# Pooled attention and a three-way maxout layer on one core: another order of all steps, and stores split by 128-token halves

## The chip, the core and the metric

The kernel runs on one core of one Trainium2 chip. The metric is the device time of one execution in microseconds (us); less is better. A core has five engines that run at once: TensorE (PE; its weight loads are shown as PEld), VectorE (DVE), ScalarE (ACT), GpSimd (POOL) and SyncE (SP). SP, POOL and ACT also issue DMAs, which share 16 DMA engines. Each engine runs its instructions in the order in which the program gives them and waits at semaphores for others.

## What is computed

```python
# B, H, S, D = 8, 8, 576, 64; pool = 8; Sp = 72
k_p = k.reshape(B, H, Sp, pool, D).mean(axis=3)
v_p = v.reshape(B, H, Sp, pool, D).mean(axis=3)
scores = scale * np.matmul(q, k_p.transpose(0, 1, 3, 2))
attn = np.exp(scores - max); attn = attn / (sum + 1e-09)
x = matmul(attn, v_p)  ->  4608 tokens x 512            # heads side by side
h = np.maximum(np.maximum(x @ w1, x @ w2), x @ w3)      # 4608 x 768
out = h @ w_out                                         # 4608 x 512
```

## The kernel before

There are two kinds of work. **Attention** goes batch by batch (8 of them, 576 tokens each), the **layer** goes by blocks of 512 tokens (9 of them, n = 0 to 8). Everything is written out by hand: the first batch and the first block stand in Python code ahead of line 869, the last output block (`out_last`) behind line 901, and all between comes from one long text, `ORDER` (L879). `run` (L829) reads it word by word and emits each step's instructions for all engines. So a word's place sets the place of its instructions on PE, DVE, ACT, POOL and SP alike.

The words, with b a batch and i a part of it:

- `<kb`, `<vb`, `<qb`: a load of 576 KB, issued by POOL (`load_k` L86, `load_v` L97, `load_q` L109). A load is made to wait for the last matmul ahead of it in the order and for the last DMA transpose ahead of it. Each of k, v and q has two buffers.
- `Kb` twice (DVE): folds eight key rows to two, a fold of 96x1536 and one of 96x768; `kb` (L207): six matmuls on PE that turn the folded keys, and four copies to `kz`.
- `Vb` seven times: four pieces `half<-vt` (L807) and two pieces `vt<-half` (L811) on POOL, then the sum `vp<-vt` on DVE. Each POOL piece waits for the last of DVE's sums that stands ahead of it (`piece`, L816).
- `qbi` (batches 1 and 2): q is transposed on PE and copied out to `qT` by ACT, or, as for every word with a star, by DVE (`move`, L77). `Tb` three times (batches 3 to 7): the same by DMA transposes, issued by SP (L305). There are two `qT` buffers.
- `sbi`, i = 0 to 8 (`scores_flat`, L237): 512 columns of scores on PE into `psf` (two buffers), exp on ACT into `et`. The first of a batch reads what the first T wrote.
- `vbi`, i = 0 to 4 (`values`, L267): eight matmuls into `pav` (one buffer), a reciprocal and a product on DVE that give `xn`, 128 tokens of x. `xbi` turns it into `xT` by PE and a copy for b up to 2; for b over 2, `v` itself issues a DMA transpose on SP (L256). `xT` is a ring of 2048 tokens.
- `p`: half a piece of block 0's output, with a copy to `osb` in every second one.
- `A` to `H` with 1 to 4 (`two_products`, L657): the hidden layer of n = 1 to 3, four matmuls of 512 or eight of 256 columns; ACT takes one product's positive part, DVE the maximum. They take and give back four PSUM banks (`take`, `give`, L524).
- Blocks 4 to 8 get the hidden layer with seven products in place of eight (`hidden_product`, L614): `1a` to `7c`, four matmuls of 256 columns each, from sums of x (`t1` to `t4`, tile `xs`, on DVE) and of the weights (`f`, `F`, on DVE, once). All output blocks go the same way (`out_product`, L712): `1d` to `7d`, ten matmuls of 256 columns, from sums of h (`u1` to `u4`, tile `hs`) and of the weights (`S`, `G`). Products 1, 2, 3, 5 and 6 are moved by ACT or, starred, by DVE; 4 and the later of 5 and 7 are added by DVE. Each block has two tiles `osb` of 2 x 128 tokens; there are three such buffers.
- `store` (L685) writes one such tile out: tokens of one position in the nine-fold interleave lie 64 to a group, so a tile holds four groups, u = 0, 1 in partition halves and m = 0, 1 in the free direction. It issues a DMA for each u, over both m where their places in the output allow it, else one for each u and m. All are on SP, in order with the transposes.

`out_last` (L745) does the last block in halves m of 128 tokens, 14 products of five matmuls, the last two being `(4, 0)` and `(4, 1)`.

Of the kernel before, what the change touches and what calls it, by code (L numbers as in the profile page):

```python
# [14 lines left out]
def kernel(  # L15
# [11 lines left out]
    nc = tc.nc  # L27
# [3 lines left out]
    B, H, S, D = q.shape  # L31
# [10 lines left out]
    NG = 9  # L42
    GS = (0, 2, 4, 6, 8, 1, 3, 5, 7)
# [18 lines left out]
    def psum(shape, dtype, name, tag, bufs):  # L62
        return pools[-1].tile(shape, dtype, name=name, tag=tag, bufs=bufs)
# [5 lines left out]
    def matmul(*args, **kw):  # L69
        latest[0] = nc.tensor.matmul(*args, **kw)  # L70
        return latest[0]
# [66 lines left out]
    for sign in (1, -1):  # L138
        nc.gpsimd.affine_select(
            out=pick, in_=pick, compare_op=ALU.is_ge, fill=0.0, base=7 * (sign < 0),  # L140
            pattern=[[sign, 6], [-8 * sign, 128]], channel_multiplier=6 * sign)
    for i in range(3):
        load_w(slice(256 * i, 256 * i + 256))
    nc.gpsimd.dma_start(
        out=wo_sb, in_=moe_w_out.rearrange("(jc p) c -> p jc c", p=128))
# [378 lines left out]
    def take(key, shape=(128, 2, 256)):  # L524
        i = free_banks.pop(0)
        taken[key] = i, psum(list(shape), F32, name="pb", tag=f"pb{i}", bufs=1)
        return taken[key][1]

    def give(key):
        free_banks.append(taken.pop(key)[0])  # L530
# [80 lines left out]
    def of(i):  # L611
        return "B" if i == 2 else "C" if i in (4, 7) else "A"
# [69 lines left out]
            nc.vector.tensor_tensor(out=hTs[n][:, j, c], in0=relus[j], in1=b, op=ALU.max)  # L682
        give("n")

    def store(e, n, j, o, c):  # L685
        for u in range(2):
            b, g = divmod(2 * (4 * n + 2 * j) + u, NG)
            pair = g + 2 < NG and GS[g + 2] == GS[g] + 4
            for m in range(0, 2, 1 + pair):
                b, g = divmod(2 * (4 * n + 2 * j + m) + u, NG)  # L690
                dst = out[S * b:S * b + S, :].rearrange("(r g) c -> r g c", g=NG)
                e.dma_start(out=dst[:, GS[g]:GS[g] + 4 * pair + 1:4, c],  # L692
                            in_=o[64 * u:64 * u + 64, m:m + 1 + pair, c])

    def out_operands(n, i, m, r):
        za, zb = PRODUCTS[i]
        c = slice(128 * m, 128 * m + 128)
        if isinstance(zb, str):
            z = int(zb[1]) - 1
            left = xs[n % 2][:, z, r, c] if r < 2 else ths[n][:, z, r - 2, c]  # L700
        else:
            at = HALF * (zb % 2) + 128 * m
            left = (tokens(NB * n + at, NB * n + at + 128)[:, 2 * (zb // 2) + r] if r < 2
                    else hTs[n][:, JH * (zb // 2) + r - 2, at:at + 128])
        h, r = (0, r) if r < 2 else (1, r - 2)
        right = so[h][:, int(za[1]) - 1, r] if isinstance(za, str) else out_w(za, h)[:, r]
        return left, right

    outs = {}
    lo, hi = slice(0, HALF), slice(HALF, C)  # L710

    def out_product(n, i):  # L712
# [27 lines left out]
        if i in (5, 7, 3) and all((n, z, "d") in done for z in (5, 7, 3)):  # L740
            store(nc.sync, n, 1, o(1), slice(0, C))
        if i in (2, 4) and all((n, z, "d") in done for z in (2, 4)):
            store(nc.sync, n, 0, o(0), slice(0, C))

    def out_last(n):  # L745

        o = sb2.tile([128, 2304], F32, name="ob", tag="et")[:, 0:2048].rearrange(
            "p (j m c) -> p j m c", j=2, m=2)
        banks, ended = {}, set()

        def product(i, m):
            f = of(i)
            if (f, m) not in banks:
                banks[f, m] = (psum([128, HALF], F32, name="oC", tag=SC[0], bufs=SC[1])
                               if f == "C" else take((f, m), (128, HALF)))
            p = banks[f, m]
            for r in range(5):
                matmul(p, *out_operands(n, i, m, r), stop=(r == 4),
                                 start=(i in FIRST and r == 0), skip_group_check=True)
            ended.add((i, m))  # L760

            def plus(j, c):
                nc.vector.tensor_tensor(out=o[:, j, m, c], in0=o[:, j, m, c],  # L763
                                        in1=banks["B" if c == lo else "C", m], op=ALU.add)

            def both_of(*parts):
                return all((z, k) in ended for z in parts for k in range(2))

            if i in (1, 5, 6, 3):
                nc.scalar.copy(out=o[:, int(i in (5, 3)), m, lo if i in (1, 3) else hi],  # L770
                               in_=p)
            elif i == 2:
                plus(0, lo)
            elif i == 4:
                plus(0, hi)
            if i in (5, 7) and (12 - i, m) in ended:
                plus(1, hi)
            if i in (2, 3):
                give((f, m))
            if i in (5, 7) and both_of(5, 7):  # L780
                store(nc.sync, n, 1, o[:, 1], hi)
            if i == 3 and both_of(3):
                store(nc.scalar, n, 1, o[:, 1], lo)
            if i in (2, 4) and both_of(i):
                store((nc.gpsimd, nc.sync)[i // 4], n, 0, o[:, 0], (lo, hi)[i // 4])

        return product

# [88 lines left out]
    for _ in range(SC[1]):  # L877
        psum([128, NB], F32, "psf", *SC)
    ORDER = """  # L879
        q12* q13 V1 p s10 s11 p* s12 V1 s13 p s14 q20* s15 V1 s16 V1 V1 p* s17 V1 s18 K2 V1  # L880
        <k3 p K2 q21 q22 <q3 V2 v10 V2 q23 V2 k2 v11 x10* <q4 p x11* v12 s20 p s21 V2 V2 V2
        s22 v13 H3 <v3 s23 s24 <k4 v14 V3 C3 s25 f x13 f B3 T3 V2 K3 x12 T3 E3 T3 G s26 K3
        s27 A4 V3 s28 t1 C4 T4 x14 v20 A3 S S T4 T4 D4 v21 x20 V3 D3 B4 x21 k3 v22 t3 u1 E4
        H4 V3 V3 <v4 v23 x22 p S G A1 H1 V3 A2 v24 s30 s31 K4 1d s32 s33 H2 s34 C1 K4 <q5
        x23* G s35 <k5 C2 t2 s36 s37 V3 t3 D1 t1 u2 s38 D2 k4 <v5 S u3 x24 G v30 E1 6d* V4
        s40 s41 t2 B1 s42 t4 v31 V4 u4 s43 V4 B2 s44 v32 s45 5d s46 F v33 s47 E2 T5 s48 V4
        V4 v34 7d u1 2d V4 V5 u3 <k6 K5 F V5 u2 3d 4d 1d K5 7d V4 t1 V5 2d <k7 6d* k5 v40 T5
        C1 V5 t4 C2 s50 s51 v41 V5 V5 T5 E1 H1 E2 v42 <q6 H2 5d u4 f B1 F D1 V5 f D2 4d B2
        K6 t2 K6 3d t3 A1 A2 F <v6 1a t1 1b <q7 s52 t2 u1 s53 v43 2a 2b K7 V6 s54 6b 6a s55
        u3 K7 s56 v44 1d s57 t4 5a s58 V6 u2 V6 2d t3 t4 3a u4 v50 k7 7b 5b* 6d T6 v51 7a 3b  # L890
        k6 4b T6 5d 4a T6 7d 1c T7 3d 2c 6c 4d t1 V6 V6 <v7 t2 5c T7 1a T7 v52 7c s60 s61 2a
        3c s62 s63 6a v53 s64 4c 1b 5a s65 s66 v54 2b 3a s70 6b 1d s67 t3 u1 u2 u3 u4 t4 s68
        5b 2d 7b V6 6d V6 V7 7a 4b 3b s71 v60 4a 1c 5d 6c* 2c s72 V7 v61 s73 7c s74 5c s75
        7d s76 V7 v62 3c s77 4c t1 4d 3d t2 u1 1d t4 u2 V7 v63 s78 t3 1a 2d u3 2a 6a 1b* 6d*
        2b v64 V7 V7 5a V7 6b 7a 3a 5d v70 5b 4a 7b v71 3b 3d u4 1c 4b 7d t1 t2 6c 7c 2c 5c
        4d 3c 1a 4c v72 1b 2a 6a 6b u1 u2 2b 5a u4 t4 v73 1d 5b u3 3a t3 6d v74 3b 2d* 7b 7a
        5d 4b 4a 7d t1 1c 3d 6c* 2c t3 4d t2 1a t4 5c 7c 2a 3c 6a 4c 1b 5a 7a 6b 2b 4a 5b 1c
        u1 3a 3b 2c u2 6c u4 u3 1d 7b 5c 6d* 4b 3c 2d 5d 7c 7d 4c 3d 4d
    """

    run(ORDER)
# [36 lines left out]
```

## Time and profile before

| | us |
|---|---|
| runs | 230.5, 229.07, 233.97; median 230.5 |
| the profiled execution | 227.75 |
| its span | 225.9, granted clock 0.997 |
| PE busy from 38.20 to 216.95 us | 174.01 of 178.75 |
| DVE busy there | 153.45 |
| ACT busy there | 113.12 |
| POOL busy there | 62.32 |

The steps of `ORDER` run from about 38 us to about 213.7. Matmuls are pipelined and the ends that the profile gives them are modelled, so PE's busy time counts some of its waiting as work; the starts of its matmuls are what tells. The page's costliest groups, by line, engine and tiles, count, busy time and mean of one:

```profile
L70 PE MATMUL pb<-xT,mw 128*128 128x256 f16 (+1 forms) x312 | 52.8, 305 | 1.2 <-DVE hT L682 1.2
L807 POOL TENSOR_TENSOR half<-vt 72x512 f32<-72x512 f16 x28 | 32.9, 1189 | 52.9 <-DMA vt<-in_v_dram 42.6
L226 ACT ACTIVATE et<-psf 72x512 f16<-72x512 f32 x63 | 35.3, 595 | 8.2 <-PE psf L70 8.1
L279 DVE TENSOR_TENSOR xn<-pav,rcp 128x512 f16<-128x512 f32 x40 | 27.7, 691 | 1.4
```

The last column is the idle time of the engine ahead of the group and what ended it. The DMA engines are over 90% busy in most of the first 60% of the span; from issue to landing the loads take 9.5 (q), 13.2 (k) and 14.1 us (v) in the median.

### The profile page before, as it was taken

The numbers are of one execution on the slowest core, as the hardware profiler recorded it, in microseconds if no ns is written. First come the engines' busy times: TensorE is split into PE (matmuls) and PEld (weight loads), VectorE is DVE, ScalarE is ACT, GpSimd is POOL, SyncE is SP. The second block draws the span as 40 slices with busy tenths as digits, with TensorE's granted clock in tenths as the row PEclk, the third lists the DMA queues.
The fourth block names the chain that finished last, engine by engine and source line by source line (L and its number), as shares of the span: only waits on it lengthen the run. The fifth ranks groups of instructions, "written<-read, shape, count | busy, mean of one in ns | idle before, by whom it ended". The sixth has DMA issues, their size and how long they took to land.

```text
span 225.9 us, 5235 instructions
## 1 busy us (share of the span) xinstructions
PE 212.3 (94%) x2046; PEld 165.7 (73%) x2046; DVE 180.2 (80%) x362; ACT 132.0 (58%) x264; POOL 82.7 (37%) x90
## 2 busy tenths in 40 slices
PE   7788999899999999998999996999999999999991
PEld 2377745558986666874679885988989898888881
DVE  3558967276999899987899965989989998988651
ACT  2267525687866887354369855957454571674230
POOL 7975300969419546459012027125140000000020
PEclk9999999999999999999999999999999999999998
DMA  6999999989999799989999999995371541430085
GB/s 166 208 197 197 204 207 205 204 160 236 151 156 132 126 163 182 151 171 194 134 211 172 155 125 171 195 156 107 70 166 36 136 105 31 115 73 0 4 229 141
DMA packets 50824, 33.57 MB, mean 149 GB/s; under 512 B 27280, under 2 KB 46352, under 8 KB 50800
## 3 DMA queue, kind: packets, MB, share of 16 engines
q0 software_dynamic: 20304, 16.98, 51.6%
q1 hardware_dynamic: 30208, 16.00, 40.8%
q8 instruction: 16, 0.26, 0.5%
q10 hardware_dynamic: 288, 0.26, 0.4%
q14 instruction: 8, 0.07, 0.1%
HBM read 34.60 MB, written 9.44 MB: 195 GB/s over the span
## 4 chain that ended last, share of the span: by engine, by line
PE 73%; DVE 11%; DMA 9%; issue 3%; ACT 1%; POOL 1%; SPq 0%; POOLq 0%; DVEq 0%; ACTq 0%
PE pb L70 54%; PE psf L70 5%; DMA qT<-qb 5%; PE pw L70 4%; PE pav L70 4%; DMA vt<-in_v_dram 4%; DVE xn L279 3%; PE pm L70 2%; PE pxt L74 1%; DVE hT L682 1%; DVE xs L537 1%; PE oC L70 1%; DVE kz L78 1%; DVE hs L537 1%; DVE rcp L277 1%
## 5 line engine op out<-in xcount | busy, mean ns | idle before, releaser
L70 PE MATMUL pb<-xT,mw 128*128 128x256 f16 (+1 forms) x312 | 52.8, 305 | 1.2 <-DVE hT L682 1.2
L70 PEld LDWEIGHTS <-mw 128*128 128x128 f16 x444 | 41.5, 98 | 16.3 <-issue 2.2
L807 POOL TENSOR_TENSOR half<-vt 72x512 f32<-72x512 f16 x28 | 32.9, 1189 | 52.9 <-DMA vt<-in_v_dram 42.6
L226 ACT ACTIVATE et<-psf 72x512 f16<-72x512 f32 x63 | 35.3, 595 | 8.2 <-PE psf L70 8.1
L279 DVE TENSOR_TENSOR xn<-pav,rcp 128x512 f16<-128x512 f32 x40 | 27.7, 691 | 1.4
L78 ACT COPY osb<-pb 128x512 f32<-128x512 f32 x25 | 14.7, 587 | 23.7 <-PE pb L70 23.7
L70 PE MATMUL psf<-qT,kz 128*128 128x256 bf16 (+4 forms) x161 | 21.3, 249 | 2.6 <-DMA qT<-qb 2.0
L636 DVE TENSOR_TENSOR ys<-ys,pb 128x512 f16<-128x512 f16 x30 | 20.3, 682 | 2.3 <-PE pb L70 2.0
L70 PEld LDWEIGHTS <-kz 128*128 128x128 bf16 x185 | 14.6, 98 | 8.5 <-issue 3.4
L70 PEld LDWEIGHTS <-hs 128*128 128x128 f16 x192 | 18.8, 98 | 2.2
L811 POOL TENSOR_TENSOR vt<-half 72x512 f16<-72x512 f32 x14 | 18.0, 1300 | 5.9 <-DVE xs L537 3.4
L692 POOL DMA_DIRECT2D out_dram<-ob x2 | 1.3, 636 | 50.1 <-DVE ob L763 50.1
L70 PE MATMUL pb<-mwo,hT 128*128 128x256 f16 (+1 forms) x120 | 19.3, 294 | 0.0
L70 PE MATMUL pb<-soh,hs 128*128 128x256 f16 x138 | 19.1, 273 | 0.0
L70 PEld LDWEIGHTS <-hT 128*128 128x128 f16 x168 | 16.3, 98 | 3.6
L78 ACT COPY pb<-pb 128x512 f32<-128x512 f32 x21 | 12.0, 575 | 10.8 <-PE pb L70 7.0
L70 PE MATMUL pav<-vp,et 72*128 72x65 f16 x320 | 17.1, 194 | 0.8 <-DVE xn L279 0.4
L78 ACT CAST ys<-pb 128x512 f16<-128x512 f32 x27 | 15.6, 593 | 3.6 <-PE pb L70 3.3
L70 PE MATMUL pb<-xs,sums 128*128 128x256 f16 x90 | 17.2, 272 | 0.1
L70 PEld LDWEIGHTS <-et 72*128 72x128 f16 x320 | 14.6, 98 | 3.5 <-DVE xn L279 1.4
L70 PE MATMUL pb<-xs,sw 128*128 128x256 f16 x90 | 17.2, 272 | 0.0
L645 ACT ACTIVATE t<-pb 128x256 f16<-128x256 f32 x30 | 11.2, 387 | 8.2 <-PE pb L70 7.8
(111 smaller groups left out, 413.0 us busy)
## 6 DMA issues: line engine op xcount, KB each, us to landing
out_dram<-osb SPq DMA_DIRECT2D x38, 128.0 KB, 2.7
ktFalse<-in_k_dram POOLq DMA_DIRECT2D x7, 576.0 KB, 13.2
qb<-in_q_dram POOLq DMA_DIRECT2D x7, 576.0 KB, 9.5
vt<-in_v_dram POOLq DMA_DIRECT2D x7, 576.0 KB, 14.1
out_dram<-osb SPq DMA_DIRECT2D x13, 256.0 KB, 3.7
mw<-in_moe_w_dram POOLq DMA_DIRECT2D x9, 256.0 KB, 9.5
ktTrue<-in_k_dram SPq DMA_DIRECT2D x3, 384.0 KB, 5.5
mwo<-in_moe_w_out_dram POOLq DMA_DIRECT2D x1, 768.0 KB, 13.3
```

The source lines that it names most:

```text
L70: latest[0] = nc.tensor.matmul(*args, **kw)
L74: latest[0] = nc.tensor.transpose(*args, **kw)
L78: (nc.vector.tensor_copy if on_vector[0] else nc.scalar.copy)(out=out, in_=in_)
L226: nc.scalar.activation(out=out, in_=in_, func=FT.Exp, scale=1.0 / 64.0)
L277: nc.vector.reciprocal(out=rcp, in_=pv[:, :, :, 64])
L279: nc.vector.tensor_tensor(out=xn, in0=pv[:, :, :, 0:D], in1=rcp.to_broadcast([128, 2, 4, D]), op=ALU.mult)
L537: t = e.tensor_tensor(out=out, in0=a, in1=b, op=op)
L636: nc.vector.tensor_tensor(out=y[:, j], in0=y[:, j], in1=bank("C", n, g), op=ALU.add)
L645: nc.scalar.activation(out=t0, in_=p[:, 0], func=FT.Relu)
L682: nc.vector.tensor_tensor(out=hTs[n][:, j, c], in0=relus[j], in1=b, op=ALU.max)
L807: yield e.tensor_tensor(out=f[:, c], in0=t[:, c, 0:4, :], in1=t[:, c, 4:8, :], op=ALU.add)
L811: yield e.tensor_tensor(out=t[:, c, 0:2, :], in0=f[:, c, 0:2, :], in1=f[:, c, 2:4, :], op=ALU.add)
```

## The change

The text `ORDER` is replaced by another order of the same 485 steps. Ten more of its copies have a star in sum (three of q, three of x, four of products), which takes them from ACT to DVE. `store` gets a form that writes 128 tokens, a whole m, with one DMA where its two groups lie side by side in the output, and the old form stays for the rest; and in the last block the half m = 0 of the last tile is stored as soon as its own product is added.

```diff
--- before.py
+++ after.py
@@ -682,7 +682,15 @@
             nc.vector.tensor_tensor(out=hTs[n][:, j, c], in0=relus[j], in1=b, op=ALU.max)
         give("n")
 
-    def store(e, n, j, o, c):
+    def store(e, n, j, o, c, parts=(0, 1)):
+        whole = [m for m in parts if 2 * (4 * n + 2 * j + m) % NG not in (4, 8)]
+        if len(whole) == len(parts):
+            for m in parts:
+                b, g = divmod(2 * (4 * n + 2 * j + m), NG)
+                dst = out[S * b:S * b + S, :].rearrange("(r g) c -> r g c", g=NG)
+                e.dma_start(out=dst[:, GS[g]:GS[g] + 3:2, c].rearrange("r u c -> u r c"),
+                            in_=o[:, m, c])
+            return
         for u in range(2):
             b, g = divmod(2 * (4 * n + 2 * j) + u, NG)
             pair = g + 2 < NG and GS[g + 2] == GS[g] + 4
@@ -781,8 +789,10 @@
                 store(nc.sync, n, 1, o[:, 1], hi)
             if i == 3 and both_of(3):
                 store(nc.scalar, n, 1, o[:, 1], lo)
-            if i in (2, 4) and both_of(i):
-                store((nc.gpsimd, nc.sync)[i // 4], n, 0, o[:, 0], (lo, hi)[i // 4])
+            if i == 2 and both_of(2):
+                store(nc.gpsimd, n, 0, o[:, 0], lo)
+            if i == 4:
+                store(nc.sync, n, 0, o[:, 0], hi, (m,))
 
         return product
 
@@ -877,25 +887,25 @@
     for _ in range(SC[1]):
         psum([128, NB], F32, "psf", *SC)
     ORDER = """
-        q12* q13 V1 p s10 s11 p* s12 V1 s13 p s14 q20* s15 V1 s16 V1 V1 p* s17 V1 s18 K2 V1
-        <k3 p K2 q21 q22 <q3 V2 v10 V2 q23 V2 k2 v11 x10* <q4 p x11* v12 s20 p s21 V2 V2 V2
-        s22 v13 H3 <v3 s23 s24 <k4 v14 V3 C3 s25 f x13 f B3 T3 V2 K3 x12 T3 E3 T3 G s26 K3
-        s27 A4 V3 s28 t1 C4 T4 x14 v20 A3 S S T4 T4 D4 v21 x20 V3 D3 B4 x21 k3 v22 t3 u1 E4
-        H4 V3 V3 <v4 v23 x22 p S G A1 H1 V3 A2 v24 s30 s31 K4 1d s32 s33 H2 s34 C1 K4 <q5
-        x23* G s35 <k5 C2 t2 s36 s37 V3 t3 D1 t1 u2 s38 D2 k4 <v5 S u3 x24 G v30 E1 6d* V4
-        s40 s41 t2 B1 s42 t4 v31 V4 u4 s43 V4 B2 s44 v32 s45 5d s46 F v33 s47 E2 T5 s48 V4
-        V4 v34 7d u1 2d V4 V5 u3 <k6 K5 F V5 u2 3d 4d 1d K5 7d V4 t1 V5 2d <k7 6d* k5 v40 T5
-        C1 V5 t4 C2 s50 s51 v41 V5 V5 T5 E1 H1 E2 v42 <q6 H2 5d u4 f B1 F D1 V5 f D2 4d B2
-        K6 t2 K6 3d t3 A1 A2 F <v6 1a t1 1b <q7 s52 t2 u1 s53 v43 2a 2b K7 V6 s54 6b 6a s55
-        u3 K7 s56 v44 1d s57 t4 5a s58 V6 u2 V6 2d t3 t4 3a u4 v50 k7 7b 5b* 6d T6 v51 7a 3b
-        k6 4b T6 5d 4a T6 7d 1c T7 3d 2c 6c 4d t1 V6 V6 <v7 t2 5c T7 1a T7 v52 7c s60 s61 2a
-        3c s62 s63 6a v53 s64 4c 1b 5a s65 s66 v54 2b 3a s70 6b 1d s67 t3 u1 u2 u3 u4 t4 s68
-        5b 2d 7b V6 6d V6 V7 7a 4b 3b s71 v60 4a 1c 5d 6c* 2c s72 V7 v61 s73 7c s74 5c s75
-        7d s76 V7 v62 3c s77 4c t1 4d 3d t2 u1 1d t4 u2 V7 v63 s78 t3 1a 2d u3 2a 6a 1b* 6d*
-        2b v64 V7 V7 5a V7 6b 7a 3a 5d v70 5b 4a 7b v71 3b 3d u4 1c 4b 7d t1 t2 6c 7c 2c 5c
-        4d 3c 1a 4c v72 1b 2a 6a 6b u1 u2 2b 5a u4 t4 v73 1d 5b u3 3a t3 6d v74 3b 2d* 7b 7a
-        5d 4b 4a 7d t1 1c 3d 6c* 2c t3 4d t2 1a t4 5c 7c 2a 3c 6a 4c 1b 5a 7a 6b 2b 4a 5b 1c
-        u1 3a 3b 2c u2 6c u4 u3 1d 7b 5c 6d* 4b 3c 2d 5d 7c 7d 4c 3d 4d
+        V1 q12* q13 V1 V1 V1 V1 G p V1 s10 s11 p* s12 <k3 s13 p q20* q21* <q3 s14 V2 q22* K2
+        K2 s15 V1 s16 p* V2 s17 s18 p k2 q23* v10 V2 p v11 V2 s20 <q4 V2 x10* p x11* v12 s21
+        f F s22 D3 <v3 V2 s23 s24 v13 G B3 s25 x12* v14 H3 V2 s26 s27 G K3 C3 S <k4 x13 t1
+        T3 A3 V3 s28 x14 t2 T3 V3 C4 v20 T3 K3 S H4 A4 v21 T4 x20* k3 D4 V3 B4 v22 u1 T4 x21
+        E3 E4 x22 T4 v23 p 1d* s30 s31 H1 v24 s32 V3 s33 H2 s34 V3 <v4 K4 2d x24* s35 C1 S
+        V3 u2 <k6 K4 <q5 t3 V3 u4 s36 s37 A1 C2 <k5 s38 t4 k4 <v5 B1 G x23* u3 V4 t1 A2 v30
+        s40 t3 V4 s41 D1 V4 s42 6d V4 S v31 s43 s44 B2 s45 v32 s46 5d s47 v33 s48 T5 7d D2
+        V4 V4 V5 v34 u1 <q6 E1 E2 V4 u2 t2 <v6 3d u3 4d T5 v40 F K5 1d K5 7d 6d u4 v41 2d V5
+        f V5 k5 V5 K6 T5 5d* v42 K6 D1 C1 F V5 s50 T6 s51 T6 C2 D2 V5 <k7 f 3d <q7 H1 H2 A1
+        A2 B1 F t3 t4 B2 E1 u1 t1 E2 4d 1a 1b t2 f v43 s52 2a s53 T6 t1 t4 t2 2b k6 v44 1d
+        s54 6b* u2 V5 6a s55 2d t3 u3 t4 s56 5b s57 V6 V6 7b 5a* s60 3b s58 4b s61 V6 V6 3a
+        V6 v50 s62 s63 7a 1c 6d* v51 2c 4a 6c* 5d 7c u4 7d 3d K7 V6 <v7 T7 v52 T7 5c 4d 3c
+        s64 t1 1a t2 s65 4c t3 u1 T7 s66 t4 1b 6a 2a s67 v53 6b s68 u2 2b 5a V6 K7 5b 1d u3
+        v54 3a 3b k7 2d 7b V7 v60 6d u4 7a s70 4b s71 v61 1c V7 s72 s73 4a 2c 5d 6c V7 s74
+        v62 s75 7d 5c* V7 s76 v63 t1 t3 s77 7c s78 3c 4d V7 t2 v64 3d V7 4c 1a 1d t4 u1 2a
+        6a 2d 1b 5a u2 u3 u4 6d V7 6b* 3a v70 2b 5b 7b 5d* 7a 3b 4b 3d 4a 1c 7d v71 t1 6c 2c
+        4d 5c t2 v72 1a 7c 3c t4 2a 6a v73 1b 4c u1 5a 2b 6b u2 v74 t3 1d 3a 5b u3 6d* 3b 7a
+        2d 1c 4a 5d 6c 7b 3d u4 4b t1 5c 7d 7c 2c t2 3c 4d 4c 1a 1b t4 2a t3 u1 6b 6a* 2b 5b
+        1d 3b 5a* u2 2d 7a 3a 1c* 4a 6d 2c 7b u4 6c u3 5d 4b 5c 7d 7c 3d 4c 3c 4d
     """
 
     run(ORDER)
```

## The prediction

> **What bounds the kernel now.** I read the page's busy shares and its chain first, then the chain in order of time, then the timeline around each place where the chain leaves TensorE (PE).
>
> ```profile
> PE 212.3 (94%) x2046; PEld 165.7 (73%) x2046; DVE 180.2 (80%) x362; ACT 132.0 (58%) x264; POOL 82.7 (37%) x90
> PE 73%; DVE 11%; DMA 9%; issue 3%; ACT 1%; POOL 1%; SPq 0%; POOLq 0%; DVEq 0%; ACTq 0%
> ```
>
> PE is busy 94% of the span and carries 73% of the chain; no other engine is near it, but VectorE (DVE) at 80% has little to spare. The change leaves PE's work as it is: the same 485 steps, the same matmuls. So only PE's idle time can be won or lost, and I measured it. The chain in order of time gives PE's price for each kind of step:
>
> ```profile
> 90.46 0.26 PE pav L70 x8
> 90.72 7.66 PE pb L70 x70
> ...
> 126.84 0.32 SPq L256
> 127.25 10.34 DMA qT<-qb
> 137.64 0.60 PE psf L70 x5
> ```
>
> 70 matmuls of 256 columns in 7.66 us are 0.109 us each. With that, a v step is 0.26 us, an s step 0.22, an x 0.22, a k 0.25, a step A to H 0.87, a hidden product (1a to 7c) 0.44, an output product (d) 1.09. I call **position** the PE work that stands in ORDER before a step; all of ORDER is 166.8 us, and the 70 matmuls of the last block add 7.6. A step's start in the trace minus its position is the time lost so far. It is 38.1 at the first p; 39.5 at v10 (47.80 less 8.3); 40.3 at v14; 40.6 at v24; 41.1 at v30; 41.8 at v34 and v40; 43.0 at v42; 43.2 at v52; 45.5 at v53; 46.2 at v74; 46.9 at the last block. So 8.8 us are lost behind 38 us, in four lumps: 2.2 up to v14, 1.5 from v14 to v40, 1.2 between v40 and v42, 2.3 between v52 and v53. The last 80 us lose 1.4 in all.
>
> The chain lines show the last lump: s60 reads what the first T6 wrote, and that transpose took 10.34 us from its issue to its landing while three loads were on the DMA engines (issued 117.54 to 119.16). T6 stands at position 82.8 and s60 at 92.3, only 9.5 us of PE work apart. The lump before it:
>
> ```profile
> 100.63 2.27 POOL L807 TENSOR_TENSOR half<-vt 72x512 f32<-72x512 f16 x2
> 101.00 2.71 DVE L537 TENSOR_TENSOR xs<-xT,xs 128x512 f16<-128x512 f16 x1
> ...
> 103.63 0.67 DVE L682 TENSOR_TENSOR hT<-t,pb 128x512 f16<-128x512 f16 x1
> ...
> 104.36 1.89 PE L70 MATMUL pb<-xT,mw 128*128 128x512 f16 x8 [0.95 <-DVE hT L682]
> ```
>
> An xs difference that mostly takes 0.42 us took 2.71 beside two fold pieces of POOL; the max behind it came late, no PSUM bank was free, and PE stood.
>
> **Part by part.** *Transposes (T).* Distances in PE work from the T step to the first s that reads it, before and after: T3 15.0 and 11.7, T4 21.8 and 17.6, T5 11.4 and 14.4, T6 9.5 and 19.3, T7 10.1 and 13.3. The smallest is now 11.7, above the 10.34 that the slowest one seen took. I take s60's wait as gone: gain 2.1 of 2.3 (bounds 0 and 2.3).
>
> *The v5 folds* no longer lie across the t steps: between v40 and v42 the queue in front of DVE is the two K folds. Of 1.2 lost I keep 0.2: gain 1.0 (bounds 0 and 1.2).
>
> *Ten more moves on DVE*, net, taken from ScalarE (ACT): three of q (0.42 to 0.49), three of x (0.42), four of products (0.69), 5.4 us by the rows. An op on DVE starts some 0.08 us before its forerunner ends, so 4.6 net: from 153.45 of the 178.75 us between 38.20 and 216.95 to 158. Cover: PE has 167 us of work there. Where that cover is gone it is charged below.
>
> *Up to v14.* In before, PE waits 0.42 for the copy of q12 (stays), 0.54 for ACT's exp beside the q copies (q20 to q23 now go to DVE, 0.49 against 0.69), and 0.34 and 0.27 around v10 and k2. The new order asks for K2 earlier, at position 5.3. k2 was issued at 23.56 and took the longest of the k loads, 22.0: it lands at 45.6, where DVE arrives near 44.6. DVE stands 1 us; its queue behind is a vp sum, an output copy, q23. K2 ends near 47.1, k2's matmuls come at about 47.6: hidden. Lost 1.2 for 2.2: gain 1.0 (bounds -0.8, if K2's wait shows in full, and 1.8).
>
> *From v14 to v24* the weight sums f, F, G, G, S and t1 are moved forward. After K2 (47.1) there are 33 DVE ops up to the end of v20's xn, 18.0 us by the rows, 15.4 net: 62.5. One of them, V2's vp sum, also needs POOL:
>
> ```profile
> 49.80 3.37 POOL L807 TENSOR_TENSOR half<-vt 72x512 f32<-72x512 f16 x3 [1.09 <-DMA vt<-in_v_dram]
> 53.13 0.78 POOL L114 DMA_DIRECT2D qb<-in_q_dram  x1
> 53.92 1.17 POOL L807 TENSOR_TENSOR half<-vt 72x512 f32<-72x512 f16 x1
> 55.04 2.49 POOL L811 TENSOR_TENSOR vt<-half 72x512 f16<-72x512 f32 x2
> 57.48 0.87 POOL L106 DMA_DIRECT2D vt<-in_v_dram  x1
> 58.68 0.41 DVE L537 TENSOR_TENSOR vp<-vt 72x512 f16<-72x512 f16 x1
> ```
>
> POOL starts V2 when v2 lands (49.8) in both orders, but now the q4 load and the v3 load (0.78 and 0.86) both stand between its pieces: 49.8 + 4 x 1.15 + 0.78 + 1.25 + 0.86 + 1.25 = 58.5, where DVE arrives some 1.5 us earlier. Behind the vp sum stand 11 ops up to v20's xn, among them G (0.54 with POOL idle, 1.79 beside it), 4.4 us net: 63.0. PE reaches v21, which needs the one pav buffer back, at 22.5 + 39.4 = 61.9. It waits 1.1, and k3 (2.2 behind K3, 6.8 before) a little: lost 1.3 for 0.3, cost 1.0 (bounds 0 and 2.7, the upper end worked out under the rivals).
>
> A rule belongs here: the Trainium skill, SBUF — State Buffer, "Who interferes with whom", says that a VectorE op with two SBUF inputs and a GpSimd op that reads SBUF exclude each other, the later one blocked for the whole of the earlier. The trace agrees in kind, but its 2.71 went past two pieces, not one. Taken at its word, with every early sum blocked by a full piece, this stage would cost 2.7; by the rows' means it costs 1.0.
>
> *v24 to v40.* The two long G sums (1.79, 1.02) and S are gone from here; k4 stands 2.4 behind K4 (3.7 before). 0.9 for 1.2: gain 0.3 (bounds -0.5, 0.9). *Behind v53*: k7 stands 2.7 behind K7's second fold (4.2 before), where DVE work up to K7 exceeds PE work by up to 3.6 us of queue: cost 0.5 (bounds 0, 0.9). x transposes keep their distance to the first t: 7.3 at least, 5.3 before.
>
> *Stores.* SP's issues of osb go from 51 to 43, 0.6 us each: hidden, since SP waits for data before most. At the end it counts:
>
> ```profile
> 219.69 3.36 SPq L692 DMA_DIRECT2D out_dram<-ob  x4
> ```
>
> Two of these four follow the last add (221.77). Now the first half leaves after its own add and one issue follows the last: gain 0.6 (bounds 0, 0.8).
>
> Sum: 2.1 + 1.0 + 1.0 - 1.0 + 0.3 - 0.5 + 0.6 = 3.5. The profiled execution took 227.75 (span 225.9, 1.85 around it): 224.3. The median of the runs, 230.5, is 1.012 of that: **227.0**.
>
> **Rivals.** *Osb jams (slower).* 5d of block 2, now moved by DVE at position 59.4 (near 101.5), reuses the osb buffer that 4d of block 1 fills; the stores stand on SP behind the first T5, which needs q5's load, now third of five issued within 6 us (v4, k6, q5, k5, v5). In before these two are 12.1 apart (52.1 and 64.2), now 6.2. If q5 lands as late as the slowest loads (24 us: 101 instead of 89), T5 adds 2.8, the v34 transposes and five stores 5, landing 3.7: 112, and DVE, and soon PE, stands 10 us: 224.3 + 10 = 234, 237 in runs. It decides from q5 landing behind 92. Against: median q landing is 9.5.
>
> *The stall moves.* q6's load stands on POOL behind the first V5 piece, which waits for v5's load (near 94). With a q landing of 20.3 and T6's 10.34 it is 126, and s60 comes at 80.8 + 42.5 = 123.3: the 2.1 is not won and some of the 1.0: 227, 229.7 in runs.
>
> *The lock.* f and F each meet a POOL piece in full (1.8 where their rows' mean is 0.85) and G too (1.79 for 0.54); 1.5 of this is time in which DVE would have stood at V2 anyway: 0.95 + 0.95 + 1.25 - 1.5 = 1.7 more, 226.0, 228.7 in runs. For it: the 2.71 above. Against: POOL has nothing to fold between V2's end and v3's landing (issued 57.3, median of the v loads 14.1). This is the case of the skill's rule.
>
> *All smooth.* Neither v21 nor k7 waits, and the stages up to v14 and from v24 to v40 reach their better bounds: 224.3 - 1.0 - 0.5 - 0.8 - 0.6 = 221.4, 224.1 in runs.
>
> **Numbers.** Forecast 0.50, smooth 0.12, stall moves 0.13, lock 0.12, jam 0.13. 2% of 230.5 is 4.6 us, about what runs that spread from 229.07 to 233.97 can tell. Under 225.9: all of smooth and a third of the forecast, 0.29. Over 235.1: the jam, 0.13. Within: 0.58. The range leaves out the jam and a little below: 223 (smooth less 0.4% of spread) to 231.5 (the moved stall plus 0.8%).
>
> **What would show it.** Right: no wait of psf for qT; xs ops near 0.42 between v40 and v42; a wait of pav at v21 for DVE xn near 62; one SP issue after the last add. Wrong: DVE idle for K2 with PE idle beside it; SP standing at a T5 or T6 for a q load while DVE waits for out_dram; a lost time behind 140 us that grows beyond 2.

## The result, and the profile after

| | before | after |
|---|---|---|
| runs, median (us) | 231.67 (229.07 to 233.97, 4 runs) | 281.14 (279.4 to 284.89, 4 runs) |
| ratio, 95% interval | | 1.221 (1.2005 to 1.2414) |
| the profiled execution | 227.75 | 282.61 |
| its span, granted clock | 225.9, 0.997 | 280.8, 0.909 |

The forecast was 227.0 and the range ended at 231.5. The change costs about 50 us. (The ratios here leave out disturbed runs that the medians still hold, so they are not quite the quotients of the medians.)

The page of the changed kernel: busy time by engine, the granted clock in 40 slices, and the shares of the chain by engine.

```profile
PE 220.3 (78%) x2046; PEld 169.7 (60%) x2046; DVE 183.0 (65%) x372; ACT 127.6 (45%) x254; POOL 82.6 (29%) x90
PEclk9999999979999999557999997799996899999755
PE 43%; DMA 31%; DVE 12%; SPq 4%; issue 2%; ACT 2%; DVEq 0%
```

No engine has more work than before to speak of (DVE 183.0 for 180.2; PE's 220.3 for 212.3 is the same 2046 matmuls, some of them at a lower clock); PE's share fell from 94% to 78%, and DMA's part of the chain rose from 9% to 31%. While PE still has work, the clock row is lowest at slices 17 and 18, from 112 to 126 us, where PE stands and the granted clock is half. The chain in order of time says what it waited for (start, length, what):

```profile
101.72 0.63 SPq L691
...
102.40 19.61 DMA out_dram<-osb
...
122.14 0.70 DVE osb L78
```

L691 is the new store. Two of them go out from 101.7 on, and the second, issued at 102.4, lands 19.61 us later. Nobody reads the output, but the buffer `osb` is needed again, by the copy of 5d of block 2. The timeline of the same stretch (start, length, engine, line, operation, count; idle time before it and what ended it in brackets):

```profile
101.72 3.19 SPq L691 DMA_DIRECT2D out_dram<-osb  x2
...
105.00 4.46 SPq L700 DMA_DIRECT2D out_dram<-osb  x3
...
109.51 9.11 SPq L305 DMA_TRANSPOSE qT<-qb  x1
...
122.14 0.69 DVE L78 COPY osb<-pb 128x512 f32<-128x512 f32 x1 [17.07 <-DMA out_dram<-osb]
...
122.89 1.01 PE L70 MATMUL pb<-sums,xT 128*128 128x256 f16 x4 [13.62 <-DVE osb L78]
```

DVE stands 17.07 us with the copy at the head of its queue, PE soon has no PSUM bank and stands 13.62 us, and on SP a single transpose, behind the stores, takes 9.11 us to issue. How fast the stores move is in the DMA view from 106 to 112 us, with no load moving until 108: mean busy share of the 16 DMA engines in tenths, and GB/s, in 40 slices.

```profile
DMA  1101111111011119953297489899999999899999
GB/s 55 55 27 55 55 55 55 55 55 55 27 55 55 55 55 93 93 78 43 62 101 101 116 162 193 170 181 216 193 208 239 208 231 231 152 196 198 137 152 161
```

A tenth of 16 engines is some two. Packet by packet, two packets of 2 KB are in flight nearly all of the time up to 108, where in the stretch before it some 20 packets of 256 bytes are. Until 105.5 us SP's queue still moves the transposes issued ahead (packets of 256 bytes), and only then does the first packet of a store start. The mean over the first 2 us of the view is about 50 GB/s, at which two stores of 256 KB take 10 us; from 108 on the loads come in beside them, and in the end it is 19.6. In a run below with the same DMAs in another form, they land in 3.1 in the median.

The other places, from the waits of all engines (us in total, times, longest):

```profile
DVE osb L78 <- DMA out_dram<-osb: 20.9, 2, 17.1
PE pb L70 <- DVE osb L78: 16.9, 2, 13.6
PE psf L70 <- DMA qT<-qb: 9.5, 3, 7.0
DVE xs L537 <- DMA xT<-xn: 5.2, 1, 5.2
```

So `osb` is waited for twice, and in between the transposes come late that stand on SP behind such stores: the one for q of batch 7, issued at 157.38 right behind two of them, lands 18.00 us later, and x's, issued at 200.19, 13.66 us later. The end of the kernel, in the timeline, and the GB/s of the DMA view from 260 to 280 us:

```profile
258.20 11.00 SPq L691 DMA_DIRECT2D out_dram<-ob  x4
...
260.08 0.97 DVE L771 TENSOR_TENSOR ob<-ob,oC 128x256 f32<-128x256 f32 x2 [0.80 <-PE oC L70]
```

```profile
GB/s 71 61 50 46 89 62 59 82 98 72 66 47 49 49 47 49 47 49 49 47 49 47 49 47 49 47 49 49 47 49 47 49 47 47 49 49 49 47 33 0
```

From the last add (261.04) to the end of the span, called the tail below, it is 19.76 us; before it was 4.12. From about 265 us on the last stores, issued by SP and ACT, move at 47 to 49 GB/s, with two or three packets in flight, however many DMAs are on their way; until then those issued by POOL go on beside them, and the sum reaches 98.

Lost time (start of a step less its position, as the prediction defined it, here with 0.4255 ns for each column of the matmuls ahead), after beyond before:

| stretch | before | after | more | what |
|---|---|---|---|---|
| first p to v42 | 5.4 | 8.2 | 2.8 | the order (below) |
| v42 to v43 | 0.0 | 18.0 | 18.0 | 5d waits for `osb`, clock halved behind it |
| v43 to v60 | 2.9 | 1.0 | -1.9 | T6 no longer waited for |
| v60 to v62 | 0.4 | 10.6 | 10.2 | T7 late |
| v62 to v74 | 0.4 | 10.8 | 10.4 | `osb` again, then x late |
| last add to the end | 4.1 | 19.8 | 15.6 | the last stores |

The sum, 55.1, less 0.3 for an earlier first p, is the difference of the spans, 54.9, up to rounding.

### The profile page after: what moved, and what is told of

Read it like the earlier page. It is cut to its first block, busy times and chain, and to the rows that moved or that the text cites. A ratio compares the mean times of both kernels' runs of the same rounds, so it can differ in the third digit from the quotient of the medians.

```text
span 280.8 us, 5236 instructions
## 1 busy us (share of the span) xinstructions
PE 220.3 (78%) x2046; PEld 169.7 (60%) x2046; DVE 183.0 (65%) x372; ACT 127.6 (45%) x254; POOL 82.6 (29%) x90
## 3 DMA queue, kind: packets, MB, share of 16 engines
q1 hardware_dynamic: 29828, 16.00, 41.7%
## 4 chain that ended last, share of the span: by engine, by line
PE 43%; DMA 31%; DVE 12%; SPq 4%; issue 2%; ACT 2%; DVEq 0%
PE pb L70 29%; DMA qT<-qb 13%; DMA out_dram<-osb 10%; DMA xT<-xn 5%; PE pw L70 3%; PE psf L70 3%; DVE xn L279 2%; DMA ktTrue<-in_k_dram 2%; PE pav L70 2%; DVE sums L537 2%; PE pm L70 2%; SPq L305 2%; DVE xs L537 1%; DVE hT L682 1%; DVE hs L537 1%
## 5 line engine op out<-in xcount | busy, mean ns | idle before, releaser
L70 PE MATMUL pb<-xT,mw 128*128 128x256 f16 (+1 forms) x312 | 57.0, 323 | 1.0 <-DVE hT L682 0.8
L70 PEld LDWEIGHTS <-mw 128*128 128x128 f16 x444 | 43.2, 102 | 19.1 <-issue 4.7
L817 POOL TENSOR_TENSOR half<-vt 72x512 f32<-72x512 f16 x28 | 32.3, 1174 | 64.1 <-DMA vt<-in_v_dram 37.5
L70 PE MATMUL psf<-qT,kz 128*128 128x256 bf16 (+4 forms) x161 | 23.2, 254 | 10.6 <-DMA qT<-qb 9.5
L70 PEld LDWEIGHTS <-xT 128*128 128x128 f16 x112 | 10.6, 98 | 21.4 <-issue 18.8
L691 POOL DMA_DIRECT2D out_dram<-ob x2 | 1.7, 838 | 65.2 <-DVE ob L771 65.2
L680 ACT ACTIVATE t<-pb 128x256 f16<-128x256 f32 (+1 forms) x24 | 11.7, 490 | 16.6 <-PE pb L70 16.4
L70 PE MATMUL pb<-sums,xT 128*128 128x256 f16 x32 | 5.4, 289 | 16.9 <-DVE osb L78 16.9
L70 PEld LDWEIGHTS <-et 72*128 72x128 f16 x320 | 15.7, 100 | 4.7 <-DVE xn L279 2.2
L78 DVE COPY osb<-pb 128x512 f32<-128x512 f32 x6 | 4.1, 690 | 22.0 <-DMA out_dram<-osb 20.9
```

The lines of the kernel that those rows point to most:

```text
L78: (nc.vector.tensor_copy if on_vector[0] else nc.scalar.copy)(out=out, in_=in_)
L680: nc.scalar.activation(out=relus[j], in_=a, func=FT.Relu)
L691: e.dma_start(out=dst[:, GS[g]:GS[g] + 3:2, c].rearrange("r u c -> u r c"), in_=o[:, m, c])
L817: yield e.tensor_tensor(out=f[:, c], in0=t[:, c, 0:4, :], in1=t[:, c, 4:8, :], op=ALU.add)
```

## The experiments

**Order or stores?** Two runs take the change apart.

First, the new order with before's `store` and `out_last`:

```diff
-    def store(e, n, j, o, c, parts=(0, 1)):
-        whole = [m for m in parts if 2 * (4 * n + 2 * j + m) % NG not in (4, 8)]
...
+    def store(e, n, j, o, c):
```

> The new order with the old stores (64 partitions to a DMA). Theory A (the new store form, whose output side begins with a dimension of 2, keeps only two DMA packets going at a time and so holds the osb buffers, the transposes and the loads): the order alone is near the kernel before, 224 to 235 us; the changed kernel's trace had lost 3.8 us more than before by v34 (94 us), ahead of any new store, so 231 to 234 is likeliest. Theory B (the order itself puts 5d of block 2, and later products, too close to the stores and behind T5 and T6): 270 to 282.

Measured: 230.58 for 227.37, ratio 1.0105 (1.0005 to 1.0205).

Second, before's order with the new `store` and `out_last`.

> The old order with the new stores. Theory A: slower by 12 to 50 us, 243 to 280, most likely 255, since the old order leaves 12 us between 4d of block 1 and the 5d that reuses its buffer where the new one leaves 6. Theory B: 229 to 233, as before.

Measured: 284.31, ratio 1.247 (1.2357 to 1.2583), tail 19.33 us: theory A, but above the 243 to 280 that it gave. Its costliest copies, by group:

```profile
L78 ACT COPY osb<-pb 128x512 f32<-128x512 f32 x25 | 14.7, 586 | 51.8 <-DMA out_dram<-osb 26.6
```

Here ACT fills the buffer and stands 26.6 us for it; in the changed kernel it is DVE. The stores alone cost all of it, in an order that nobody fitted to them, and the order alone about 1%.

**Is it the one DMA for 128 tokens?** The same halves at the same moments, but a DMA for each 64 partitions, in both orders:

```diff
-                e.dma_start(out=dst[:, GS[g]:GS[g] + 3:2, c].rearrange("r u c -> u r c"),
-                            in_=o[:, m, c])
+                for u in range(2):
+                    e.dma_start(out=dst[:, GS[g] + 2 * u, c], in_=o[64 * u:64 * u + 64, m, c])
```

> The changed kernel with its half stores as they are, but each written by two DMAs of 64 partitions instead of one of 128 that begins with a dimension of 2: 14 more issues on SP, the same bytes, the same places. Theory A: as the order alone, within 2 us of it. If instead the jam comes from when the halves are stored and what they wait for (theory B), 270 to 282.

> The old order with half stores of two 64-partition DMAs each, and the last block's first half stored as soon as it is added. Theory A: the kernel before, less the 0.6 us forecast for the last store, 229.5 to 232. Theory B: the same.

Measured: 232.01, ratio 1.0184 (1.0137 to 1.0231), with the new order; 230.04, ratio 1.0112 (1.007 to 1.0153), with the old one. All of the 50 us is back but the order's part, and the split itself costs about 1%: eight issues on SP at the end take 4.96 us, and the tail is 4.8, 0.7 more than before; what the rest is wasn't shown. So the moment at which the halves are stored wasn't the trouble; the form of the DMA was, its size or its pattern.

**What in the form?** A store of m writes `2x64x512`: u in front, 64 rows behind. Three runs vary it. The first keeps the 2 in front and cuts each DMA into two of 256 columns:

```diff
+                for w in range(2):
+                    d = slice(c.start + (c.stop - c.start) // 2 * w,
+                              c.start + (c.stop - c.start) // 2 * (w + 1))
+                    e.dma_start(out=dst[:, GS[g]:GS[g] + 3:2, d].rearrange("r u c -> u r c"),
+                                in_=o[:, m, d])
```

> The changed kernel with each 256 KB half store cut into two DMAs of 128 partitions x 256 columns: as many DMAs, each as large, as in the halves written by 64 partitions (232 us), but the output side still begins with the dimension of 2. If the dimension of 2 is the cause (two packets at a time, whatever the DMA's size): 275 to 290. If a 256 KB DMA is simply too large, or SP needs more issues to keep the queue full: 229 to 236. By the Trainium skill, DMA: Bandwidth & Descriptors, section Why a DMA increments its semaphore by 16 and not by 1, the number of DMA engines that a transfer uses is the largest up to 16 that divides the slowest dimension of both its sides, so here 2: it expects the first.

Measured: 284.47, ratio 1.2437 (1.208 to 1.2794). So the size, 256 KB or 128, isn't it, and twice the DMAs in flight bring nothing: they share what one had.

The second leaves one DMA for 128 partitions but puts the 64 in front. Since that puts tokens in each other's places, it is a probe and no version to use:

```diff
-                e.dma_start(out=dst[:, GS[g]:GS[g] + 3:2, c].rearrange("r u c -> u r c"),
-                            in_=o[:, m, c])
+                e.dma_start(out=dst[:, GS[g]:GS[g] + 3:2, c], in_=o[:, m, c])
```

> The changed kernel with each half store as one DMA of 128 partitions to the same rows of the output, but with the rows taken in the other order, so that its output side begins with the dimension of 64 and the 2 comes second. Tokens of the two groups change places in the output. Same DMAs, same bytes, same places of issue. If the dimension of 2 in front is the cause: 227 to 234, as the order alone or the halves by 64. If 128 partitions in one DMA, or the time at which halves are stored, is the cause: 275 to 290.

Measured: 231.25, ratio 1.0083 (1.0017 to 1.0149). Its page lists the same 21 DMAs, with a landing time in us at the end that the changed kernel's page leaves blank; the tail is 3.34 us, against 4.12 of before:

```profile
out_dram<-osb SPq DMA_DIRECT2D x21, 256.0 KB, 3.1
```

Its packets of 2 KB take 0.084 us each in the median, as in the changed kernel from 106 to 108 us, but 16 to 20 of them are in flight from 103 to 104 us, where there it was two.

The third has the new order, with the new form in the last block alone:

```diff
-        if len(whole) == len(parts):
+        if len(whole) == len(parts) and n == LAST:
```

> The new order with the old stores for all blocks but the last, which uses the new ones (eight DMAs of 128 KB). From the last add to the end the changed kernel took 19.8 us, the order alone 4.2. If the slow stores add up by their bytes (1 MB at the 48 GB/s of the changed kernel's last stage is 22 us from the first issue): the order alone plus 15.5, 244 to 248. If the end of the changed kernel is only late because earlier stores are still queued: 230 to 234.

Measured: 246.52, ratio 1.0778 (1.0326 to 1.1229), tail 19.8 us. So the last block's stores account for some 16 us of the 50 by themselves, as the table of lost time has it (15.6), and the rest comes from the earlier blocks.

**The 2 in front, or the zigzag of addresses?** Two runs on the kernel before, without any of the change, settle that. In the last block each store of 64 partitions is cut by rows:

```diff
-                e.dma_start(out=dst[:, GS[g]:GS[g] + 4 * pair + 1:4, c],
-                            in_=o[64 * u:64 * u + 64, m:m + 1 + pair, c])
+                for rows in (slice(0, 62), slice(62, 64)) if n == LAST else (slice(0, 64),):
+                    e.dma_start(out=dst[rows, GS[g]:GS[g] + 4 * pair + 1:4, c],
+                                in_=o[64 * u + rows.start:64 * u + rows.stop, m:m + 1 + pair, c])
```

> The kernel before, order and all; only in the last block is each store of 64 partitions cut by rows into one of 62 and one of 2. The same tokens go to the same places, and no output pattern has a short dimension in front of the 64: only the number of rows changes. If the number of engines of a store is the largest number up to 16 that divides its count of rows on both sides (the Trainium skill, DMA: Bandwidth & Descriptors, "Why a DMA increments its semaphore by 16 and not by 1"), 62 rows and 2 rows both go over two engines: the last 0.8 to 1.0 MB leave at about 48 GB/s as in the changed kernel, the tail behind the last add is 15 to 20 us where before it is 4.1, and the time is 11 to 16 us above before. Rival, that the changed stores are slow for the zigzag of their addresses (u ahead of r): nothing here has it, so the tail is that of the cut into 48 and 16, about 5 us, and the time within 2 us of before.

> The control of the run with 62 and 2 rows: the same cut with 48 and 16 rows, both of which 16 divides. The same number of DMAs and issues. Both theories: all engines take part, the tail grows by some of the four additional issues behind the last add (0.6 us each), to 4.5 to 5.5 us, and the time is within 2 us of before. If the cut itself were what is slow, by the number of DMAs in flight, this run would show the long tail too.

Measured: 244.51 with 62 and 2 rows, ratio 1.0669 (1.0537 to 1.0801); 228.12 with 48 and 16, ratio 0.9949 (0.99 to 0.9998). The timelines of the end, first 62 and 2, then 48 and 16:

```profile
219.57 15.29 SPq L693 DMA_DIRECT2D out_dram<-ob  x8
```

```profile
219.44 4.12 SPq L693 DMA_DIRECT2D out_dram<-ob  x8
```

And the GB/s of the run with 62 and 2 rows, from 222 to 242 us:

```profile
GB/s 85 106 130 19 21 33 74 93 62 45 43 47 41 49 45 49 49 47 47 49 49 45 49 49 49 49 47 47 49 47 47 49 49 49 39 25 10 0 0 0
```

The last adds end at 221.7 and 221.5 us and as many DMAs are issued; with 62 and 2 rows the tail is 20.1 us, from 227 us on at 41 to 49 GB/s, as in the changed kernel, with 48 and 16 rows it is 4.7. The zigzag isn't needed, then: the number that leads the pattern is enough. The Trainium skill, DMA: Bandwidth & Descriptors, "Why a DMA increments its semaphore by 16 and not by 1", has the rule: a DMA goes over as many engines as the largest number up to 16 that divides the size of the slowest dimension, other than 1, on both sides. 64, 48 and 16 give 16 engines; 62 rows give 2, and so does a 2 in front. The two packets in flight agree. For DMAs issued by SP or ACT the page also says that these are the lowest-numbered engines; the run that was cut by columns, with twice the DMAs and the same time, agrees, and so does the end of the changed kernel, where SP's and ACT's stores together have no more than three packets in flight.

**What the order is worth.** In the run with the order alone, T6 is waited for no longer, and 0.1 us is lost between v40 and v42 instead of 1.3. What took it back is in its timeline:

```profile
107.09 3.37 POOL L807 TENSOR_TENSOR half<-vt 72x512 f32<-72x512 f16 x3
108.43 2.46 DVE L537 TENSOR_TENSOR kp<-halfh 96x768 f16<-96x768 f16 x1
...
112.01 2.32 PE L70 MATMUL pb<-xT,mw 128*128 128x512 f16 x10 [2.71 <-DVE hT L682]
```

and in its chain, where the first T3 is on its way:

```profile
61.15 15.80 DMA qT<-qb
```

The second fold of K6, 0.54 us with POOL idle, takes 2.46 beside the V5 pieces, and PE waits 2.71. One run moves three `V5` behind the second `K6` in that kernel:

```diff
...
-v41 2d V5 f V5 k5 V5 K6 T5 5d* v42 K6 D1 C1 F V5 s50
+v41 2d f k5 K6 T5 5d* v42 K6 V5 V5 V5 D1 C1 F V5 s50
...
```

> The order alone (230.6 us, 1.0105 of before) with three V5 folds of POOL moved behind the second K6 fold of DVE. In the order alone that fold took 2.46 us for 0.54 beside three POOL pieces back to back, and PE stood 2.7 us for a bank. If the exclusion of POOL's pieces and DVE's two-input sums cost the order that time: 2 to 3 us less, ratio 0.99 to 1.00 of before. If PE would only wait for the next thing (the adds queued on DVE): ratio 1.005 to 1.015.

Measured: 229.0 for 229.01, ratio 1.0028 (0.9993 to 1.0064). Its timeline:

```profile
107.43 0.69 DVE L78 COPY osb<-pb 128x512 f32<-128x512 f32 x1 [2.90 <-DMA out_dram<-osb]
...
109.60 0.54 DVE L537 TENSOR_TENSOR kp<-halfh 96x768 f16<-96x768 f16 x1
```

The fold is back at 0.54, but the copy of 5d ahead of it, which stood 2.23 us with the order alone, stands 2.90, here for `osb`, with old stores; PE still waits 1.46. Level with before, and between the two forecasts: from v42 to v43 this trace loses 2.0 us where the order alone lost 2.8, so taking the fold out of the lock was worth less than the 2 to 3 us hoped for. What else holds PE there wasn't tried.

The last two runs give before's order its T6 early, without the rest; the first of them:

```diff
...
-6d* k5 v40 T5 C1 V5 t4 C2
+6d* k5 <q6 v40 T5 C1 V5 t4 C2
...
-v42 <q6 H2 5d
+v42 H2 5d
...
-<q7 s52 t2 u1 s53 v43 2a 2b K7 V6 s54
+<q7 T6 s52 t2 u1 s53 T6 v43 2a 2b K7 V6 T6 s54
...
```

(the three T6 of old, behind 6d, 4b and 4a, are gone). This is the h1 that the second expectation names. The second moves `t4` ahead of k5 as well: `6d* t4 k5 <q6 v40 T5 C1 V5 C2`.

> The kernel before with the q6 load moved ahead of v40 and the three T6 transposes moved some 9 to 10 us of PE work ahead (19 us from the first T6 to s60, as in the changed order). If the one good step of the changed order is T6: the wait of 2.0 to 2.3 us for qT goes, ratio 0.985 to 0.995 of before. If the transposes collide there with other loads or stores, 0.995 to 1.005.

> The same, and t4 of block 2 moved ahead of k5 and v40, so that DVE does it before the POOL pieces that locked it out for 2.3 us, and the pieces behind it wait for it. If that lock cost 1.1 us of PE in the kernel before: ratio 0.980 to 0.990. If the lock only meets the next DVE sum instead: as h1.

Measured: 231.64, ratio 1.0066 (1.0014 to 1.0118), and 230.27, ratio 1.0014 (0.9968 to 1.006). Neither gains. In their traces (executions of 232.23 and 231.09 us) PE no longer waits for T6, but it does for T5 near 120 us, 1.8 and 2.4, and for T3 near 76 us, 0.6 and 0.8, in code that is the same in all three kernels; in the first an xs sum between v40 and v42 takes 3.38 us beside POOL. So single landings differ from run to run by as much as the gain. No version tried is one to take for before: the 0.9949 of the run with 48 and 16 rows has nothing in its trace to carry it, whose span isn't shorter (226.2 for 225.9) and whose tail is longer (4.7 for 4.1).

## Why the prediction was wrong

**The step that failed** is the one on the stores: "SP's issues of osb go from 51 to 43, 0.6 us each: hidden". It priced the new store by its issue on SP and took for granted that the landing stays what it was; the jam rival even counts with "landing 3.7". The landing was 19.6 us at 101.7. Of the 54.9 us of span, 15.6 are the tail and some 35 are waits for `osb`, transposes behind such stores, and the half clock after them (v42 to v43 and v60 to v74: 18.0 + 10.2 + 10.4, less 3.3 that the order alone loses more than before there); the other 4 are about what the order alone costs. How these 35 split among the three was read from the waits, not tried one by one; whether another `osb` buffer would cover them wasn't tried. The rule that two runs now bear out could have been weighed beforehand, as the pattern's front is written in the diff: `"r u c -> u r c"` with two u. Of the signs of being wrong that the prediction names, the one that came is the lost time behind 140 us: it grows by some 22 from v43 to v74, where 2 was allowed.

**Osb jams.** The place was right, 5d of block 2 near 101.5, and so was the end of the way: DVE standing for the buffer, PE soon after. What held the buffer wasn't: q5's load landed at about 95 us, before SP came to that T5 at 96.5, and the stores went out 2 us behind their data; it was their landing. The small form, 2.90 us with old stores, showed in the run with the V5 moved.

**The other terms** are a few us or less, and some of them differ by as much from one execution to the next, so the table gives them from eight traces in which no store over two engines stands ahead of the last block. Four have the old order: before, its stores cut to 62 and 2 rows, to 48 and 16 rows, and the halves by 64. Four have the new one: the order alone, 64 in front, the new form in the last block alone, and V5 moved. Lost time in us, lowest to highest of the four:

| stretch | old order | new order | forecast |
|---|---|---|---|
| up to v14, from the span's start | 40.3 to 40.5 | 41.4 to 41.7 | gain 1.0 |
| v14 to v24 | 0.2 to 0.5 | 0.9 to 1.1 | cost 1.0 |
| v24 to v40 | 1.2 to 2.4 | 1.2 to 3.0 | gain 0.3 |
| v40 to v42 (V5) | 0.4 to 2.1 | 0.1 | gain 1.0 |
| v42 to v43 | 0.0 | 2.0 to 2.8 | none |
| v52 to v53 (T6) | 0.1 to 5.1 | 0.1 | gain 2.1 |
| v53 to v74 | 0.7 to 1.6 | 0.6 to 1.4 | cost 0.5 |

**T6** (2.1). The wait is gone with the new order, as forecast. But its size was that of one execution: with the old order PE waits there 2.0 us in before's trace, 3.2 with halves by 64, 0.7 with 62 and 2 rows and not at all with 48 and 16, and these last two are before's kernel up to the last block.

**The v5 folds** (1.0): right where they were. They were only put elsewhere: v42 to v43 loses 2.0 to 2.8 where the old order loses nothing. The sum had no term for V5 beside K6 or for 5d's copy behind a store.

**Up to v14** (gain 1.0). Here the forecast had the wrong sign: the new order is 0.9 to 1.4 us later at v14 in every trace. K2 cost PE no wait, but the early f and F did, one step sooner than predicted. The timeline of the changed kernel:

```profile
53.95 2.12 DVE L537 TENSOR_TENSOR sums<-mw 128x768 f16<-128x768 f16 x1
54.36 1.29 POOL L821 TENSOR_TENSOR vt<-half 72x512 f16<-72x512 f32 x1
...
57.30 0.43 PE L70 MATMUL pav<-vp,et 72*128 72x65 f16 x8 [1.75 <-DVE xn L279]
```

pav waits for xn at v14, 57.3, not at v21 near 62. F takes 2.12 where it takes 0.55 with POOL idle, longer by a whole POOL piece (1.29) and some. The lock rival had counted 1.8 for it; in the other three traces of the new order in the table that have this wait F takes 2.0 to 2.1, too, and PE stands 1.15 to 1.34. (The order alone lacks the wait; its trace is 1.3 us late already at the first p, which the others are not.)

**v14 to v24** (cost 1.0): a cost of 0.4 to 0.9 in these traces; the changed kernel's own lost 2.4 there.

**T distances, v24 to v40** (gain 0.3). "The smallest is now 11.7, above the 10.34 that the slowest one seen took" failed: T3 took 15.65 in the changed kernel and 15.80 with the order alone. The bound rested on one landing; before's own trace has 14.2 for another. Neither a gain nor a cost shows in the whole stretch: the two ranges overlap.

**Last store** (0.6): right by the run with 64 in front, 0.8 (tail 3.34 for 4.12), and of no use with two engines.

So the order alone, 2.9 us better by the sum without the last store, is about 1% worse (1.0005 to 1.0205): its gains at V5 and T6 are there, the second of a size that changes from run to run, and go back up to v24 and between v42 and v43.

## What to carry to other kernels

Read the leading size of both sides of every DMA that a change writes, and the number of engines that it makes, before its size or its number of issues: 62 rows, or two groups in front, left two of 16 engines at work here; 64, or 48 and 16, did not. Price a store by its landing, and name who needs its buffer and what stands behind it on its queue; nobody reads an output, but 5d stood 17 us for one. A wait for a DMA's landing is a range and not a number: look at it in several traces before counting it as a gain. And a gain won by moving a step is only won if what comes into its place has been costed too: two folds moved out of one lock went into another.

## What the runs showed of the hardware that had not been expected

- Stores led by 2 groups, 62 rows or 2 rows, issued by SP and ACT, move at about 48 GB/s in all, one or many of them; the issue of such DMAs holds SP too (15.29 us for eight with 62 and 2 rows, 4.12 for eight with 48 and 16).
- PE's clock after the long stop, in windows of the changed kernel (length; busy time of PE, PEld, DVE, ACT and POOL, with counts; granted clock; DMA share; GB/s):

```profile
126.00:130.00 4.00, 4.00 (x10) 1.41 (x10) 1.49 (x3) 0.60 (x1) 2.27 (x2) 0.50 1.13 192
130.00:134.00 4.00, 4.00 (x18) 1.72 (x17) 2.41 (x6) 1.19 (x2) 0.44 (x1) 0.93 0.80 156
```

  The clock is still 0.50 from 126 to 130, though PE has been at work since 122.9; 512 columns take 0.40 us there (10 matmuls in 4.00), 0.24 in before (8 in 1.89). In this window alone that is 1.6 us lost beyond the stop itself.
- A sum on DVE stayed blocked past more than one POOL operation in a row: 2.71 us past two (before), 2.46 past the last two of three (order alone), 3.38 past two (T6 early), for 0.42 and 0.54 otherwise. Nor does it need to come second: F's record (53.95) begins before that of the POOL piece (54.36; POOL's times are rough), and it is F that takes 2.12.
